# Two chunks of keys per product with v, longer prices for GpSimd and VectorE in the planner, and a new set of offsets, in a fused attention and two-MLP kernel

## The chip, the cores and the metric

The kernel runs on one core of one Trainium2 chip. The time is the device time of one execution in microseconds. Six views of the hardware occur below: PE is TensorE's matmul, PEld its weight load, DVE is VectorE, ACT is ScalarE, POOL is GpSimd and SP is SyncE, which issues all DMAs.

## The reference

Attention over 4 batches of 12 heads (448 positions, 64 channels), with an RMS norm on q and k, and then two gated MLPs without a residual, all in fp32:

```python
q_n, k_n = rmsnorm(q, g_q), rmsnorm(k, g_k)
scores = matmul(q_n, k_n.T) / sqrt(64)
attn = exp(scores - max(scores)); attn = attn / (sum(attn) + 1e-9)
x = matmul(attn, v)                    # -> 1792 tokens x 768
x = ((x @ w_a) * (x @ w_b)) @ w_out    # 768 -> 1536 -> 768
h = x @ w_in                           # 768 -> 2048
return (h * clip(h + 3, 0, 6) / 6) @ w_out2
```

## The kernel before

Products of the MLPs are made of fp32r matmuls on a value split in two: a high part (ACT rounds it) and a low part (the rest, a subtraction on DVE or POOL). Three matmuls of 128x128 by 448 columns make one exact product. Attention runs pair by pair of heads (`pair`, 24 pairs in four batches of six): scores for seven chunks of queries (L533, L534), exponentials on ACT, then the scaled probabilities `p` are turned by PE (L571, L585 to L588) into `pt`, whose copies out of PSUM go to ACT or DVE (L408, L412), and `value` (L598) multiplies them with `rv`. There are four chunks of keys, k = 0 to 3, so four `value` steps per pair; each is one matmul for the lower and one for the upper head of the pair, 64 columns of weights each, in plain fp32, which the profiler records as four matmuls. The last chunk has 64 rows per head. There are two `pt` buffers.

From about 80 us on, the MLP work of the batches that are done is laid between the attention of the later ones: `layer` for the first half of the tokens (L691 to L693). From about 816 us on only MLP is left: `layer7` (L964), which makes each 2x2 block product out of seven instead of eight; its weight sums (L922), its low halves (L397) and its output sums (L972) are DVE and POOL work. The first such layer ends and the second begins at about 1053 us.

The order on every engine is made at build time by the class `Plan`. Each operation is added with a due time, a cost per engine that may run it, and the tiles that it reads and writes. `run` then steps through planned time: each engine takes the operation with the earliest due time that is ready and whose buffers are free; an operation that several engines can do is taken by the first one listed, or by another when that one is busy for more than `LW` ns or the operation is late by more than a number in `LB` or `LF`. Costs that are marked as shared keep DVE and POOL from running at the same planned time. What comes out is one fixed list for each engine; on the chip, semaphores make an instruction wait where its inputs are late.

The tables of numbers at the top are the due times: `T` and `TQ` (start and pace of each batch), `R` (start and rate of each MLP stage), `OA` to `OD` (steps of a pair), `OW`, `LEAD` (weights of `layer`), `LW7`, `LX7` (how far ahead of a product `layer7` loads, sums and splits). `on_pool` and `on_dve` are the planned costs.

Of the kernel before, what the change touches and what calls it, by code (L numbers as in the profile page):

```python
# [19 lines left out]
NB, NH, S, D = 4, 12, 448, 64  # L20
# [5 lines left out]
PH = DM // 2  # L26
# [1 line left out]

T = (6.793, 78.0, 255.0, 440.0)
TQ = (1.45, 3.637, 4.75, 4.118)
R = ((85.0, 1.515), (255.0, 1.267), (411.278, 1.34), (703.581, 1.0), (943.0, 1.0))


BS = ((2, 3, 4), (1, 2, 3, 4), (2, 3, 4), (3, 4))
# [18 lines left out]

LB = (
    (548.658, 276.261, 561.206), (548.658, 402.965, 561.206), (548.658, 402.965, 561.206),
    (735.919, 402.965, 561.206),  # L60
)
LF = (
    (548.658, 402.965, 561.206), (548.658, 402.965, 561.206), (548.658, 402.965, 561.206),
    (548.658, -149.766, 561.206),
)
LW = 112.877


OA = (-7.027, -5.631, -5.6, -5.526, -4.903, -4.8, -4.475, -4.381)
OB = (-4.0, -2.7, -3.2, -2.3, -2.579, -2.6, -2.385)  # L70
OC = (0.0, -0.24, 0.482, 0.457, 4.632, 4.519)
UT = 5.13
UK = 2.0
OD = (0.4, 1.972, 3.0)


LEAD = 21.868
OW = (-9.089, -9.23, 1.129, 3.002, -1.607)
AFTER = 2.571


SLICE = (3, 3, 2)
# [4 lines left out]


MM = 206.7
LW7 = (34.0, 25.0, 20.0, 18.0)  # L90

SLICE7 = ((3, 3), (3, 3, 2))
XLEAD, XSTEP = -14.0, 3.7
LX7 = (20.0, 19.0, 18.5)


def piece_order(up, down, n, k):
# [49 lines left out]
class Plan:  # L149
# [16 lines left out]
    def add(self, due, cost, fn, reads=(), writes=(), after=()):  # L166


        o = Op()
        o.due, o.fn, o.idx = due * 1000.0, fn, len(self.ops)  # L170
        o.late = self.late
        o.cost = {e: c if isinstance(c, tuple) else (c, e == "G") for e, c in cost.items()}
        o.succ, o.need, o.ready = [], 0, 0.0
        o.bufs = []
        deps = {id(d): d for d in after}
        for k in reads:
            if k in self.last:
                deps[id(self.last[k])] = self.last[k]
        for k in writes:
            if k in self.last:  # L180
                deps[id(self.last[k])] = self.last[k]
            for d in self.readers.pop(k, ()):
                deps[id(d)] = d
        for k in reads:
            self.readers.setdefault(k, []).append(o)
        for k in writes:
            self.last[k] = o
        seen = set()
        for k in (*reads, *writes):
            b = k[0] if isinstance(k, tuple) else k  # L190
            if isinstance(b, Buf) and id(b) not in seen:
                seen.add(id(b))
                o.bufs.append(b)
                b.left += 1
        deps.pop(id(o), None)
        for d in deps.values():
            d.succ.append(o)
        o.need = len(deps)
        self.ops.append(o)
        return o  # L200

    def run(self, engines):
# [22 lines left out]
        while True:  # L225
            again = True
            while again:
                again = False
                for e in queue:
# [3 lines left out]
                    for key in queue[e]:  # L233
# [7 lines left out]
                        first = next(iter(o.cost))  # L241
                        if e != first and now < o.due + o.late[e] and free[first] <= now + LW:
                            continue
# [66 lines left out]


def on_pool(n):
    return (146 + 2.11 * n, True)


@with_exitstack
def fused_kernel(ctx: ExitStack, tc: tile.TileContext, nat, qt, gs_in, wpk, outT):
    nc = tc.nc
    V, A, G, SP = nc.vector, nc.scalar, nc.gpsimd, nc.sync
# [70 lines left out]
    def bank(role, ids, ordered=True):  # L390
        return Buf([banks[i] for i in ids], lines.setdefault(role, []) if ordered else None)

    plan = Plan()
    add = plan.add
# [23 lines left out]
    def pair(n0):  # L418
# [3 lines left out]
        b, h = divmod(n0, NH)  # L422
        plan.late = dict(zip("VAG", LB[b]))
        t0, q = T[b] + 4 * TQ[b] * h, TQ[b]
        lower, upper = slice(0, D), slice(D, P)

        def at(u):
            return t0 + q * u

        def at_chunk(j):  # L430
# [4 lines left out]
        rn, rv, sq, kc, ms, rstd, nt, sums, rs = [  # L435
            buf(k) for k in ("rn", "rv", "sq", "kc", "ms", "rstd", "nt", "sums", "rs")]
# [5 lines left out]
        for i, (lo, hi, who) in enumerate(alike):  # L442
            add(at(-10.7 + i), {"SP": 90 * (hi - lo)}, lambda e, lo=lo, hi=hi: e.dma_start(
                out=rn.t[:, lo:hi].rearrange("p c d -> p (c d)"), in_=nat[n0 // 2][:, lo * D:hi * D]),
                writes=[(rn, k) for k in who])
        for i in range(2):
            add(at(-8.9 + (4 * i if n0 else 0)), {"SP": 640}, lambda e, i=i: e.dma_start(out=rqs[i].t, in_=qt[n0 + i]),
                writes=[rqs[i]])
        add(at(-2.0), {"SP": 640}, lambda e: e.dma_start(
            out=rv.t.rearrange("p c d -> p (c d)"), in_=nat[n0 // 2][:, 14 * D:]), writes=[rv])  # L450
        for i, (lo, hi, who) in enumerate(alike):
            n, sl = (hi - lo) * D, slice(lo, hi)
            x, y, z, m, sk = [[(o, k) for k in who] for o in (rn, rstd, nt, ms, sq)]

            def square(e, sl=sl):
# [5 lines left out]
            cost = {"V": (on_dve(n), True), "A": on_act(n), "G": on_pool(n)}  # L461
            add(at(OA[0]), {k: cost[k] for k in ("VAA"[i] if n0 == 0 else SQ[b])}, square,
                reads=x, writes=sk)
            add(at(OA[1]), {"V": on_dve(n)}, lambda e, sl=sl: e.reduce_sum(out=ms.t[:, sl], in_=sq.t[:, sl], axis=AX.X),
                reads=sk, writes=m)
# [3 lines left out]
                reads=m, writes=y)  # L469
            add(at(OA[4]), {"A": 100}, lambda e, sl=sl: e.activation(rstd.t[:, sl], rstd.t[:, sl], AF.Exp, scale=-0.5),  # L470
                writes=y)
# [4 lines left out]
                reads=y, writes=z)  # L476
            add(at(OA[7]), {"V": 80}, lambda e, sl=sl: e.scalar_tensor_tensor(
                out=rstd.t[:, sl], in0=nt.t[:, sl], scalar=1.5, in1=rstd.t[:, sl], op0=ALU.add, op1=ALU.mult),
                reads=z, writes=y)
        for i in range(2):  # L480
            kcl, n, c0 = kcols[i], 4 - i, 4 * i
# [6 lines left out]
                reads=[y], writes=[(rn, f"{i}k")])  # L488
# [4 lines left out]
                reads=[(rn, f"{i}k"), (kc, i, 0)], writes=[(kc, i, 1)])  # L493
            tk = bank("t", BT[b], False)

            def turn_k(e, i=i, tk=tk):
# [14 lines left out]
                reads=[tk], writes=[kks[i]])  # L511

            def qhigh(e, i=i):
# [6 lines left out]
                reads=[rqs[i], "gg"], writes=[qhs[i]])  # L520
            add(at(OB[6] + 4 * i), {"V": (596, True)}, lambda e, i=i: e.scalar_tensor_tensor(
                out=qls[i].t[:, own_q[i]], in0=rqs[i].t, scalar=gg[:, 0:1], in1=f32(qhs[i].t[:, own_q[i]]), op0=ALU.mult, op1=ALU.subtract),
                reads=[rqs[i], qhs[i], "gg"], writes=[qls[i]])
        ps = []
        for j in range(NCK):
# [10 lines left out]
            u = j * 8 / NCK  # L536
# [20 lines left out]
        for j in range(0 if LATE[b] else NCK):  # L557
            opts = {"V": (363, True), "G": (617, True), "A": 560}
            add(at(4 + OC[5] + 0.15 * j), {k: opts[k] for k in NORM[b][j // 2]}, lambda e, j=j: norm(e, j),
                reads=[rs], writes=[ps[j]])  # L560
        pv = bank("v", BV[b])
        for k in range(4):
            pt = buf("pt")
            u = 4 + UT + k * UK
            if k < 3:
                for i, n in enumerate((4, 3)):
                    t = bank("t", BT[b], False)

                    def turn_p(e, k=k, i=i, n=n, t=t):
                        for c in range(n):  # L570
                            e.transpose(t.t[:, c * P:(c + 1) * P], ps[4 * i + c].t[:, k * P:(k + 1) * P], ident)  # L571

                    add(at(u + 0.5 * UK * i), {"PE": 109 * n}, turn_p, writes=[t, (pt, i)],
                        reads=["ident", *ps[4 * i:4 * i + n]])
                    cost = copy_ps(n * P)
                    add(at(u + 0.5 * UK * i + OD[0]), {x: cost[x] for x in PT[b]}, lambda e, i=i, n=n, t=t, pt=pt: copy(
                        e, pt.t[:, 4 * P * i:(4 * i + n) * P], t.t[:, :n * P]), reads=[t], writes=[(pt, i)])
                own = slice(0, P), slice(0, P)
                at_v, cols = (k, 4 + k), (0, S)
            else:  # L580
                t = bank("t", BT[b], False)

                def turn_rest(e, t=t):
                    for c in range(4):
                        e.transpose(t.t[:, c * P:(c + 1) * P], ps[3 + c].t[:, S - P:], ident)  # L585
                    for c in range(3):
                        e.transpose(t.t[lower, c * P:(c + 1) * P], ps[c].t[:, S - D:], ident)  # L587
                    e.transpose(t.t[lower, 3 * P:S], ps[3].t[lower, S - D:], ident[lower, lower])  # L588

                add(at(u), {"PE": 820}, turn_rest, reads=["ident", *ps], writes=[t, (pt, 0)])  # L590
                cost = copy_ps(4 * P)
                add(at(u + OD[0]), {x: cost[x] for x in PT[b]}, lambda e, t=t, pt=pt: copy(
                    e, pt.t[:, :4 * P], t.t), reads=[t], writes=[(pt, 0)])
                own, at_v, cols = (lower, upper), (3, 3), (0, D)

            def value(e, k=k, pt=pt, own=own, at_v=at_v, cols=cols):
                for i, rows in enumerate((lower, upper)):
                    e.matmul(pv.t[rows, :S], rv.t[own[i], at_v[i]], pt.t[own[i], cols[i]:cols[i] + S],  # L598
                             start=k == 0, stop=k == 3)

            add(at(u + OD[1]), {"PE": 930}, value, reads=[(pt, 0), (pt, 1), rv], writes=[pv])
        m, due = h // 2, at(u + OD[2])
        if LATE[b]:
            rb, eb = bank("t", BT[b], False), buf("tmp", "e")
# [17 lines left out]
        if b < GB:  # L622
            add(due, {"A": 424}, lambda e: e.activation(xx[:, m, b, 0], pv.t[:, :S], AF.Copy),
                reads=[pv], writes=[("xh", m, b)])
            add(due + 0.2, {"V": 535}, lambda e: sub(e, xx[:, m, b, 1], pv.t[:, :S], f32(xx[:, m, b, 0])),
                reads=[pv, ("xh", m, b)], writes=[("xl", m, b)])
            if n0 >= GHEAD - 4:
                tails.append(plan.ops[-1])
        else:
            add(due, {"A": 424, "V": 535}, lambda e: copy(e, xf[:, m, b - GB], pv.t[:, :S]),  # L630
                reads=[pv], writes=[("xf", m, b - GB)], after=tails)
# [246 lines left out]
    def layer7(no, ids, clock, late, finish):  # L878
# [223 lines left out]
        writes=["gg"])  # L1102
    add(0.2, {"V": 80}, lambda e: e.tensor_scalar(
        out=gg[:, 0:1], in0=gg[:, 0:1], scalar1=float(D) ** -0.5, scalar2=None, op0=ALU.mult), writes=["gg"])
    for k, sl in (("0", slice(S, 4 * P)), ("1", slice(0, D))):
        for x in ("qh", "ql"):
            t = K[x + k][0].tile
# [12 lines left out]

    layer(0, (0,), BM[0], pace(*R[0]), SLICE[0], LF[0])
    layer(0, (1,), BM[1], pace(*R[1]), SLICE[1], LF[0])
    ends[:] = [add(690.0, {"G": (1, False)}, switch, after=ends)]
    first_x = x_maker(xf, lambda m, bi: ("xf", m, bi), R[3][0], ends, held)
    layer(1, (0, 1), BM[2], pace(*R[2]), SLICE[2], LF[2], lambda k, due: first_x(XORDER[k], due))
    layer7(0, BM[3], pace(*R[3]), LF[2], x_maker(acc, lambda m, bi: ("acc", m, bi), R[4][0]))
    layer7(1, BM[4], pace(*R[4]), LF[3], lambda mb, due: put(mb[0], GB + mb[1], due))
    with tc.manual_schedule():
# [52 lines left out]
```

## Time and profile before

| what | value |
|---|---|
| median of 3 runs | 1277.68 us (1277.48 to 1277.71) |
| the profiled execution | 1274.44 us, its span 1272.7 us |
| PE busy, PEld busy | 97%, 82% of the span |
| DVE, ACT, POOL busy | 81%, 53%, 20% |
| granted TensorE clock, mean | 0.999 |

The span runs from the first to the last instruction; 1.7 us lie outside of it. A matmul's record overlaps the next one's, so the pace of PE is read from the distance of starts, and its waits from the idle time that is put down to a releaser.

### The profile page before, as it was taken

Reading aid. Unit: us, or ns where it says so; the run is one execution under the profiler, and the core shown is the slowest. Engines: PE = TensorE matmul, PEld = TensorE weight load, DVE = VectorE, ACT = ScalarE, POOL = GpSimd, SP = SyncE. Lnnn points to the kernel's source line nnn. Section 1 sums busy time; section 2 is a strip of 40 time slices with the busy share of each in tenths; the row PEclk is TensorE's granted clock in tenths of the full one; section 3 lists DMA queues with packets and bytes.
Section 4 is the critical chain, followed back from the end, with each engine's and each line's share of the span. In section 5 each row is a group of like instructions: output and inputs, shape, how many; then the busy total and the mean of one; then the engine's idle time right before and its main releaser. Section 6 shows DMA issues by size and latency. Waiting matters only on the chain.

```text
span 1272.7 us, 18366 instructions
## 1 busy us (share of the span) xinstructions
PE 1236.0 (97%) x6342; PEld 1039.3 (82%) x6342; DVE 1027.8 (81%) x1859; ACT 668.9 (53%) x1428; POOL 258.0 (20%) x281
## 2 busy tenths in 40 slices
PE   5999999999999999999999999999999999899998
PEld 3668777777988887888778878899899888799897
DVE  8999998997557798877878775876877799977977
ACT  7996766677235564654767643522422245534432
POOL 4331102212000021110121000522212234413131
PEclk9999999999999999999999999999999999999999
DMA  6456676765687587656646353655355445255433
GB/s 203 139 187 227 215 257 203 281 228 197 216 274 241 173 314 252 207 177 227 205 142 209 122 173 108 232 155 162 121 176 158 132 129 182 85 178 157 131 107 123
DMA packets 107853, 235.57 MB, mean 185 GB/s; under 512 B 9200, under 2 KB 74096, under 8 KB 107760
## 3 DMA queue, kind: packets, MB, share of 16 engines
q1 hardware_dynamic: 107760, 234.39, 56.2%
q8 instruction: 50, 0.82, 0.3%
q14 instruction: 43, 0.35, 0.1%
HBM read 162.01 MB, written 72.35 MB: 184 GB/s over the span
## 4 chain that ended last, share of the span: by engine, by line
PE 73%; DVE 15%; DMA 5%; issue 4%; ACT 2%; POOL 1%; SPq 0%; DVEq 0%; POOLq 0%; ACTq 0%
PE bank L964 26%; PE bank L691 10%; PE bank L693 10%; PE bank L692 10%; PE bank L598 5%; PE bank L571 4%; DMA wst<-in_w_dram 3%; PE bank L533 3%; PE bank L534 2%; DVE act L397 2%; DVE w L397 2%; DMA rn<-in_nat_dram 1%; PE bank L498 1%; DVE wf L649 1%; DVE acc L972 1%
## 5 line engine op out<-in xcount | busy, mean ns | idle before, releaser
L691 PE MATMUL bank<-xx,w 128*128 128x448 f32 x480 | 182.3, 380 | 1.1 <-DVE act L397 0.9
L693 PE MATMUL bank<-xx,w 128*128 128x448 f32 x480 | 175.5, 366 | 0.0
L692 PE MATMUL bank<-xx,w 128*128 128x448 f32 x480 | 175.4, 365 | 0.0
L964 PE MATMUL bank<-act,w 128*128 128x448 f32 x711 | 155.0, 366 | 6.0 <-DVE acc L972 4.1
L964 PEld LDWEIGHTS bank<-act,w 128*128 128x128 f32 x711 | 133.0, 188 | 18.9 <-ACT w L899 4.4
L964 PE MATMUL bank<-xx,w 128*128 128x448 f32 x612 | 132.1, 366 | 0.8 <-DVE acc L972 0.8
L691 PE MATMUL bank<-act,w 128*128 128x448 f32 x336 | 127.7, 380 | 2.6 <-DVE act L397 1.9
L673 ACT ACTIVATE w<-wf 128x768 fp32r<-128x768 f32 x104 | 85.6, 840 | 78.9 <-PE bank L692 64.8
L964 PEld LDWEIGHTS bank<-xx,w 128*128 128x128 f32 x612 | 114.9, 188 | 10.8 <-DVE acc L972 1.2
L693 PE MATMUL bank<-act,w 128*128 128x448 f32 x336 | 122.8, 366 | 0.0
L692 PE MATMUL bank<-act,w 128*128 128x448 f32 x336 | 122.7, 365 | 0.0
L397 DVE TENSOR_TENSOR w<-wf,w 128x384 fp32r<-128x384 f32 x185 | 101.3, 584 | 18.9 <-ACT w L673 15.8
L797 DVE TENSOR_TENSOR acc<-bank,acc 128x448 f32<-128x448 f32 x120 | 74.3, 622 | 48.4 <-PE bank L693 48.0
L539 DVE TENSOR_REDUCE nm<-bank 128x1 f32<-128x448 f32 x168 | 102.4, 618 | 13.0 <-PE bank L534 8.3
L543 ACT ACTIVATE p<-bank,nm,rstd 128x448 f32<-128x448 f32 x131 | 94.5, 724 | 27.5 <-PE bank L587 17.0
L408 ACT ACTIVATE pt<-bank 128x512 f32<-128x512 f32 (+1 forms) x131 | 71.4, 547 | 61.7 <-PE bank L571 51.4
L397 POOL TENSOR_TENSOR w<-wf,w 128x384 fp32r<-128x384 f32 x48 | 55.0, 1154 | 230.4 <-ACT w L673 224.8
L691 PEld LDWEIGHTS bank<-xx,w 128*128 128x128 f32 x480 | 90.2, 188 | 12.6 <-DVE act L397 1.7
L693 PEld LDWEIGHTS bank<-xx,w 128*128 128x128 f32 x480 | 90.1, 188 | 7.7
L692 PEld LDWEIGHTS bank<-xx,w 128*128 128x128 f32 x480 | 90.4, 188 | 6.2
L598 PE MATMUL bank<-pt,rv 128*64 128x448 f32 (+1 forms) x384 | 92.5, 563 | 0.5 <-DVE act L397 0.5
L964 PE MATMUL bank<-xt,w 128*128 128x448 f32 x405 | 89.7, 368 | 3.1 <-DVE xf L412 3.1
(214 smaller groups left out, 2487.4 us busy)
## 6 DMA issues: line engine op xcount, KB each, us to landing
wst<-in_w_dram SPq DMA_DIRECT2D x68, 768.0 KB, 5.9
split<-w SPq DMA_DIRECT2D x102, 384.0 KB, 3.7
w<-split SPq DMA_DIRECT2D x85, 384.0 KB, 3.9
kept<-wf SPq DMA_DIRECT2D x68, 384.0 KB, 3.0
wf<-kept SPq DMA_DIRECT2D x65, 384.0 KB, 4.2
wst<-kept SPq DMA_DIRECT2D x39, 384.0 KB, 3.6
rq<-in_qt_dram SPq DMA_DIRECT2D x48, 224.0 KB, 3.4
rn<-in_nat_dram SPq DMA_DIRECT2D x23, 448.0 KB, 4.1
```

The costliest lines, as they stand in the source:

```text
L397: e.tensor_tensor(out=out, in0=a, in1=b, op=ALU.subtract)
L408: A.activation(out, in_, AF.Copy)
L539: add(at(u + OC[1]), {"V": 531}, lambda e, s=s, nm=nm: e.tensor_reduce(out=nm.t, in_=s.t[:, :S], axis=AX.X, op=ALU.max, negate=True), read ...
L543: add(at(u + OC[3]), {"A": 704}, lambda e, j=j, s=s, nm=nm, p=p: e.activation(p.t, s.t[:, :S], AF.Exp, bias=nm.t, scale=rstd.t[:, qcol[j]: ...
L571: e.transpose(t.t[:, c * P:(c + 1) * P], ps[4 * i + c].t[:, k * P:(k + 1) * P], ident)
L598: e.matmul(pv.t[rows, :S], rv.t[own[i], at_v[i]], pt.t[own[i], cols[i]:cols[i] + S], start=k == 0, stop=k == 3)
L673: add(due - LEAD + OW[2], {"A": on_act(DM)}, lambda e: e.activation(w.t[:, 0], wf.t.bitcast(F32), AF.Copy), reads=both, writes=[(w, 0, 0), ...
L691: e.matmul(ps, w.t[:, 0, wsl], xh, start=start, stop=False)
L692: e.matmul(ps, w.t[:, 0, wsl], xl, start=False, stop=False)
L693: e.matmul(ps, w.t[:, 1, wsl], xh, start=False, stop=stop)
L797: add(due, {"V": 535}, lambda e, m=m, bi=bi, ps=ps: e.tensor_tensor(out=acc[:, m, bi], in0=ps.t[:, :S], in1=acc[:, m, bi], op=ALU.add), re ...
L964: e.matmul(out, w.t[:, a, chunk(c)], x, start=first and j + k == 0, stop=j + k == n + 1, skip_group_check=not first)
```

## The change

`value` now takes two chunks: for k = 0 and 2 the buffer is only noted, and at k = 1 and 3 one step is added that makes the four matmuls of both, with a planned cost of 1750 ns (two steps of 930 ns before). It reads both `pt` buffers. In `add`, every cost on DVE is multiplied by 1.03; in `on_pool`, operations of 384 and more columns cost 1.25 times as much. The tables of due times and the limits `LB`, `LF`, `LW` have new values. No arithmetic is added or taken away.

```diff
-T = (6.793, 78.0, 255.0, 440.0)
+T = (6.793, 74.014, 253.235, 440.0)
...
-R = ((85.0, 1.515), (255.0, 1.267), (411.278, 1.34), (703.581, 1.0), (943.0, 1.0))
+R = ((85.0, 1.74), (255.0, 1.196), (411.278, 1.34), (703.581, 1.0), (932.169, 1.0))
...
-LW = 112.877
+LW = 161.162
...
-LW7 = (34.0, 25.0, 20.0, 18.0)
+LW7 = (26.748, 25.0, 29.204, 19.253)
...
+        if "V" in o.cost:
+            o.cost["V"] = o.cost["V"][0] * 1.03, o.cost["V"][1]
...
-    return (146 + 2.11 * n, True)
+    return ((146 + 2.11 * n) * (1.25 if n >= PH else 1.0), True)
...
+        pts = []
         for k in range(4):
...
-            def value(e, k=k, pt=pt, own=own, at_v=at_v, cols=cols):
-                for i, rows in enumerate((lower, upper)):
-                    e.matmul(pv.t[rows, :S], rv.t[own[i], at_v[i]], pt.t[own[i], cols[i]:cols[i] + S],
-                             start=k == 0, stop=k == 3)
-
-            add(at(u + OD[1]), {"PE": 930}, value, reads=[(pt, 0), (pt, 1), rv], writes=[pv])
+            pts.append((k, pt, own, at_v, cols))
+            if k % 2 == 0:
+                continue
+
+            def value(e, two=tuple(pts)):
+                for k, pt, own, at_v, cols in two:
+                    for i, rows in enumerate((lower, upper)):
+                        e.matmul(pv.t[rows, :S], rv.t[own[i], at_v[i]], pt.t[own[i], cols[i]:cols[i] + S],
+                                 start=k == 0, stop=k == 3)
+
+            add(at(u + OD[1]), {"PE": 1750}, value, reads=[rv, *((t[1], x) for t in pts for x in range(2))], writes=[pv])
+            pts = []
```

**The place of `value` on PE.** The rows are the second pair of heads, whose v is `rv_257`, at its first two chunks; `kk`, `qh`, `ql` belong to scores, `ident` to the turning of probabilities, `identr` to that of keys. Before:

```order
L533 MATMUL bank_67<-kk_265,qh_261 128x448
L534 MATMUL bank_67<-kk_265,ql_263 128x448
L598 MATMUL bank_70<-pt_273,rv_257 64x448 x2
L533 MATMUL bank_65<-kk_265,qh_261 128x448
L534 MATMUL bank_65<-kk_265,ql_263 128x448
L598 MATMUL bank_70<-pt_274,rv_257 64x448 x2
L571 MATMUL bank_63<-ident,xf 128x128 x4
```

And now:

```order
L529 MATMUL bank_67<-kk_265,qh_261 128x448
L530 MATMUL bank_67<-kk_265,ql_263 128x448
L494 MATMUL bank_69<-identr,kc_259 128x64
L494 MATMUL bank_69<-identr,kc_259 128x128 x3
L612 MATMUL bank_63<-ident,rs_229 64x128 x6
L612 MATMUL bank_63<-ident,rs_229 64x64 x2
L600 MATMUL bank_64<-pt_273,rv_257 64x448 x2
L600 MATMUL bank_64<-pt_274,rv_257 64x448 x2
L529 MATMUL bank_65<-kk_265,qh_261 128x448
L530 MATMUL bank_65<-kk_265,ql_263 128x448
```

The two chunks stand next to each other, and other work has moved out from between them. Over the whole program the 96 chunk products of PE stand in 90 places before (84 alone, six in twos) and in 48 now, always two together.

**Where the second MLP begins, on PE.** `act` are the last output products of the first `layer7`, `xx` the first products of the second one, which read what DVE sums and splits out of the former. Before, from about 1047 us on:

```order
L964 MATMUL bank_65<-act_241,wb_6817 128x448 x3
L964 MATMUL bank_65<-act_242,w_237 128x448 x3
L964 MATMUL bank_65<-act_243,w_238 128x448 x3
L964 MATMUL bank_64<-act_241,wb_6817 128x448 x3
L964 MATMUL bank_64<-act_242,w_237 128x448 x3
L964 MATMUL bank_64<-act_243,w_238 128x448 x3
L964 MATMUL bank_63<-xx,w_238 128x448 x9
L964 MATMUL bank_64<-xx,w_237 128x448 x9
L964 MATMUL bank_65<-xx,w_239 128x448 x9
```

And now:

```order
L967 MATMUL bank_66<-xx,w_238 128x448 x9
L967 MATMUL bank_63<-act_241,wb_6859 128x448 x3
L967 MATMUL bank_63<-act_242,w_237 128x448 x3
L967 MATMUL bank_63<-act_243,w_238 128x448 x3
L967 MATMUL bank_67<-xx,w_237 128x448 x9
L967 MATMUL bank_64<-act_241,wb_6859 128x448 x3
L967 MATMUL bank_64<-act_242,w_237 128x448 x3
L967 MATMUL bank_64<-act_243,w_238 128x448 x3
L967 MATMUL bank_63<-xx,w_239 128x448 x9
L967 MATMUL bank_65<-act_241,wb_6859 128x448 x3
```

Three products of the new layer now stand between the last three of the old one.

**POOL in the middle of the second MLP** (the products that run from 1138 to about 1168 us before). `ws`, `wst`, `wf` are sums of weights, `w` and `wb` low halves of weights, `act` and `tmp` activations. Before, these are all:

```order
L397 TENSOR_TENSOR act_241<-tmpx_6826,act_241 128x448
L397 TENSOR_TENSOR tmp_247<-tmp_247,tmpx_6826 128x448
L397 TENSOR_TENSOR wb_6818<-wst_232,wb_6818 128x384
L397 TENSOR_TENSOR act_242<-xf,act_242 128x448
```

And now, in the same stretch:

```order
L925 TENSOR_TENSOR ws_6862<-wst_232 128x384
L393 TENSOR_TENSOR w_240<-ws_6862,w_240 128x384
L925 TENSOR_TENSOR ws_6861<-wf_234,wst_232 128x384
L393 TENSOR_TENSOR act_241<-tmpx_6868,act_241 128x448
L925 TENSOR_TENSOR wf_234<-ws_6861,wf_234 128x384
L393 TENSOR_TENSOR tmp_247<-tmp_247,tmpx_6868 128x448
L393 TENSOR_TENSOR w_237<-ws_6863,w_237 128x384
L925 TENSOR_TENSOR ws_6863<-wst_232 128x384
L393 TENSOR_TENSOR w_239<-ws_6863,w_239 128x384
L925 TENSOR_TENSOR ws_6862<-wf_235,wst_232 128x384
L393 TENSOR_TENSOR act_242<-xf,act_242 128x448
```

Sums and low halves of weights have come over from DVE. Counted over the program, 79 instructions leave DVE (1859 to 1780) and 77 come to POOL (279 to 356); 65 of them are such sums and halves of 384 columns (DVE 365 to 300, POOL 115 to 180).

## Rows read from the trace of the kernel before

**Rows 1.** The page, busy time of each engine.
```profile
PE 1236.0 (97%) x6342; PEld 1039.3 (82%) x6342; DVE 1027.8 (81%) x1859; ACT 668.9 (53%) x1428; POOL 258.0 (20%) x281
```

**Rows 2.** The page, chain that ended last, by engine.
```profile
PE 73%; DVE 15%; DMA 5%; issue 4%; ACT 2%; POOL 1%; SPq 0%; DVEq 0%; POOLq 0%; ACTq 0%
```

**Rows 3.** Stretches: length, busy time of PE, PEld, DVE, ACT, POOL, clock.
```profile
30.00:100.00 70.00, 70.00 (x478) 44.48 (x477) 66.47 (x131) 62.89 (x167) 23.76 (x42) 1.00 0.53 164
100.00:250.00 150.00, 147.31 (x763) 118.85 (x762) 138.57 (x258) 101.79 (x218) 25.38 (x30) 1.00 0.69 235
```

**Rows 4.** Timeline of PE, one chunk alone: start, length, instruction.
```profile
65.95 0.36 PE L533 MATMUL bank<-kk,qh 128*128 128x448 f32 x1
66.15 0.37 PE L534 MATMUL bank<-kk,ql 128*128 128x448 f32 x1
66.45 0.97 PE L598 MATMUL bank<-pt,rv 128*64 128x448 f32 x4
67.35 0.47 PE L533 MATMUL bank<-kk,qh 128*128 128x448 f32 x1
67.67 0.37 PE L534 MATMUL bank<-kk,ql 128*128 128x448 f32 x1
```

**Rows 5.** Timeline of PE, chunks 2 and 3 together.
```profile
59.81 0.37 PE L534 MATMUL bank<-kk,ql 128*128 128x448 f32 x1
60.10 1.87 PE L598 MATMUL bank<-pt,rv 128*64 128x448 f32 x8
61.91 0.55 PE L609 MATMUL bank<-ident,rs 128*64 128x128 f32 x6
```

**Rows 6.** Timeline of PEld, the second chunk of rows 5.
```profile
61.01 0.19 PEld L598 LDWEIGHTS bank<-pt,rv 64*64 64x64 f32 x4 [0.70 <-DVE nm L539]
```

**Rows 7.** Timeline of PE, chunks 0 and 1 together.
```profile
678.38 1.72 PE L598 MATMUL bank<-pt,rv 128*64 128x448 f32 x8
680.04 0.66 PE L571 MATMUL bank<-ident,p 128*128 128x128 f32 x4
```

**Rows 8.** Stretches, columns as in rows 3, around the MLPs' seam.
```profile
999.80:1109.10 109.30, 99.97 (x479) 90.45 (x478) 103.58 (x158) 51.94 (x101) 48.12 (x39) 0.98 0.44 134
934.10:999.80 65.70, 65.70 (x326) 60.88 (x325) 42.39 (x72) 14.18 (x28) 8.96 (x8) 1.00 0.57 163
```

**Rows 9.** Timeline of PE at three waits (idle time, releaser in brackets).
```profile
1025.42 0.44 PE L964 MATMUL bank<-act,w 128*128 128x448 f32 x1 [2.47 <-DVE acc L972]
...
1055.69 2.50 PE L964 MATMUL bank<-xx,w 128*128 128x448 f32 x11 [0.84 <-DVE acc L972]
...
1091.62 2.70 PE L964 MATMUL bank<-xt,w 128*128 128x448 f32 x9 [3.10 <-DVE xf L412]
1094.12 3.00 PE L964 MATMUL bank<-xx,wb 128*128 128x448 f32 x9
1096.96 2.02 PE L964 MATMUL bank<-act,w 128*128 128x448 f32 x9
```

**Rows 10.** DVE groups from 1000 to 1110 us: count, busy time, mean.
```profile
L397 DVE TENSOR_TENSOR act<-xf,act 128x448 fp32r<-128x448 f32 x16 | 13.8, 887 | 0.8 <-ACT act L1039 0.6
...
L397 DVE TENSOR_TENSOR act<-tmpx,act 128x448 fp32r<-128x448 f32 x5 | 5.7, 1136 | 0.1
```

**Rows 11.** Groups over the whole run, columns as in rows 10.
```profile
L397 DVE TENSOR_TENSOR w<-wf,w 128x384 fp32r<-128x384 f32 x185 | 101.3, 584 | 18.9 <-ACT w L673 15.8 <-ACT w L899 1.6
...
L397 DVE TENSOR_TENSOR act<-bank,act 128x448 fp32r<-128x448 f32 x56 | 34.6, 617 | 4.2 <-ACT act L700 3.8
...
L408 ACT ACTIVATE pt<-bank 128x512 f32<-128x512 f32 x73 | 43.4, 594 | 42.4 <-PE bank L571 32.3 <-PE bank L588 9.7
...
L397 POOL TENSOR_TENSOR w<-wf,w 128x384 fp32r<-128x384 f32 x48 | 55.0, 1154 | 230.4 <-ACT w L673 224.8 <-PE bank L534 2.6 <-ACT rstd L468 1.7
```

**Rows 12.** Timeline of DVE beside POOL's next row.
```profile
1021.23 1.57 DVE L397 TENSOR_TENSOR act<-xf,act 128x448 fp32r<-128x448 f32 x1
```

**Rows 13.** Timeline of POOL there.
```profile
1020.85 1.47 POOL L397 TENSOR_TENSOR tmp<-tmpx,tmp 128x448 f32<-128x448 f32 x1 [2.10 <-DVE tmpx L397]
```

More of the change, by code (lines that the diff above doesn't have):

```diff
@@ L26 @@
 PH = DM // 2
-T = (6.793, 78.0, 255.0, 440.0)
-TQ = (1.45, 3.637, 4.75, 4.118)
-R = ((85.0, 1.515), (255.0, 1.267), (411.278, 1.34), (703.581, 1.0), (943.0, 1.0))
+T = (6.793, 74.014, 253.235, 440.0)
+TQ = (1.436, 3.637, 4.788, 4.218)
+R = ((85.0, 1.74), (255.0, 1.196), (411.278, 1.34), (703.581, 1.0), (932.169, 1.0))
 BS = ((2, 3, 4), (1, 2, 3, 4), (2, 3, 4), (3, 4))
@@ L54 @@
 LATE = (True, False, False, False)
[L58 to L65, printed above, removed]
-LW = 112.877
-OA = (-7.027, -5.631, -5.6, -5.526, -4.903, -4.8, -4.475, -4.381)
-OB = (-4.0, -2.7, -3.2, -2.3, -2.579, -2.6, -2.385)
-OC = (0.0, -0.24, 0.482, 0.457, 4.632, 4.519)
+LB = ((344.344, 276.261, 561.206), (548.658, 402.965, 561.206), (548.658, 402.965, 561.206), (606.623, 311.013, 561.206))
+LF = ((548.658, 394.053, 761.141), (548.658, 402.965, 561.206), (548.658, 402.965, 561.206), (553.891, -149.766, 668.974))
+LW = 161.162
+OA = (-7.027, -5.631, -5.6, -5.311, -5.026, -4.8, -4.475, -4.381)
+OB = (-4.77, -2.7, -3.245, -2.3, -2.091, -2.6, -2.386)
+OC = (0.104, -0.677, 0.482, 0.457, 4.632, 4.519)
 UT = 5.13
@@ L77 @@
 LEAD = 21.868
-OW = (-9.089, -9.23, 1.129, 3.002, -1.607)
-AFTER = 2.571
+OW = (-8.493, -9.23, 1.129, 3.002, -1.61)
+AFTER = 2.346
 SLICE = (3, 3, 2)
@@ L89 @@
 MM = 206.7
-LW7 = (34.0, 25.0, 20.0, 18.0)
+LW7 = (26.748, 25.0, 29.204, 19.253)
 SLICE7 = ((3, 3), (3, 3, 2))
 XLEAD, XSTEP = -14.0, 3.7
-LX7 = (20.0, 19.0, 18.5)
+LX7 = (10.733, 19.0, 18.5)
 def piece_order(up, down, n, k):
```

## The prediction

> **What bounds the kernel now.** I read the page first, then the chain, then stretches, then single rows. PE is busy 97% of the span, and 73% of the chain that ended last is PE, 15% DVE [rows 1, 2]. So a nanosecond taken from PE's list counts, unless another engine sets the pace where it is taken. By stretches: from 30 to 250 us PE is busy 217.3 of 220 us, but DVE is nearly as full: 66.5 of 70 us, then 138.6 of 150 [rows 3]. The one long stretch where PE clearly loses time is 999.8 to 1109.1 us, the end of the first and the start of the second MLP: DVE is busy 103.6 of 109.3 us and PE waits for it, up to 3.1 us at once [rows 8, 9]. At the pace of the stretch ahead of it, 65.7 us for 326 matmuls or 0.2015 us each, its 479 matmuls would take 96.5 us; 12.8 us are lost there. Part of that is the pace itself: the granted clock of the stretch is 0.98, and after the 3.1 us wait two products of nine matmuls take 2.50 and 2.84 us from start to start [rows 9] where 9 x 0.2015 is 1.81, so 1.7 us went on a lower clock.
>
> **Two chunks in one step.** This is PE work, and the rows price it. Two neighbouring score matmuls start 0.20 us apart. Ahead of a chunk that stands alone the distance is 0.30, and the chunk takes 0.90 us to the next start [rows 4]; so one alone costs 0.90 + 0.10 = 1.00, two alone 2.00 us. Chunks 2 and 3 together (the second has the shape of 64 rows, [rows 6]) start 0.29 after their predecessor and take 1.81: 1.90 us, saving 0.10. Chunks 0 and 1 together take 1.66; with the same 0.09 ahead 1.75, saving 0.25 [rows 5, 7]. In other words a stop on each change of kind is paid once, and two chunks of 128 rows also run into each other. Of the 24 couples of each sort, two of the first and four of the second already stand together before (one of each in [rows 5, 7]). The change therefore gives 22 x 0.25 + 20 x 0.10 = 5.5 + 2.0 = **7.5 us** less PE work. Another 0.12 us goes with each chunk whose next matmul is a score (0.32 instead of 0.20 between the L533 and L534 behind it, [rows 4]); which neighbours come is a matter of the new order, and I count nothing for it (at most 42 x 0.12 = 5 us, likely 1).
>
> What could take it back: a couple must wait for both copies out of PSUM, and both `pt` buffers stay taken until it is done, so the copies for chunks 2 and 3 start later. Behind a waiting couple stand scores and turned probabilities of the next pair, and MLP matmuls. In the new order the couples stand further behind the turning that feeds them than the single chunks did: at least about ten short matmuls or scores lie between, where before it was as few as five. Ten of these last about 2 us, and the copy takes ACT 0.594 us [rows 11]. I cost this wait at nothing; if the cover is gone at every couple, 48 times 0.3 us (the size of a stop at a change of kind) is 14 us, the far end.
>
> **New prices and offsets.** They add no work; they choose engines and order. 65 sums and low halves of weights go from DVE to POOL. At 0.584 us each that is 38 us less on DVE, and at 1.154 us 75 us more on POOL [rows 11], which was busy 258 of 1272.7 us [rows 1]. DVE's relief only shows where PE waits for DVE. Between the same PE products I counted the instructions in both orders and priced them with their mean durations: in the tight stretch (999.8 to 1109.1 us) DVE gets 106.4 us of work before and 107.8 us after, POOL 48.0 before and 40.4 after. So the relief is elsewhere: 10 us in 100 to 225 us, 11 us in 1138.2 to 1176.6 us. Less POOL work in the tight stretch helps DVE a little, since DVE is held up beside it: the same subtraction that takes 617 ns with its source in PSUM takes 887 and 1136 ns there with its source in SBUF [rows 10, 11], 16 x 0.27 + 5 x 0.52 = 6.9 us on 48.1 us of POOL; 7.6 us less POOL is 1.1 us less of that. It cancels the 1.4 us more. The tight stretch should then stay as long as it is, but for the new order at its seam: three products of the new layer stand between the last of the old one, so that PE has work while DVE makes the first operands, and the wait of 0.84 us at 1055.69 us [rows 9] has cover. I take **1.0 us** for it (with the restart of PE behind it). Bounds: all 12.8 us of the stretch gained, or the three longest waits of rival C added.
>
> For the rest of the list (first 30 us, short waits in the attention) the trace gives no sign; I take zero, and 3 us either way.
>
> The sum, against the profiled execution: 1274.4 - 7.5 - 1.0 = 1265.9 us. The median of the runs is 3.2 us above that execution, so 1277.7 - 8.5 = **1269.2 us**.
>
> **The rivals.**
>
> A. *The tight stretch dissolves.* The planner now believes that DVE and POOL take longer (1.154 us for a POOL row, where 0.956 was planned and 1.195 now), so it may place what PE needs earlier, and DVE waits less beside POOL. For it: 6.9 us of holding up, POOL work down by 7.6 us, and the seam woven. Against it: the DVE work itself is not less. At its full size, 1277.7 - 7.5 - 12.8 = 1257.4 us; at half, 1264.
>
> B. *DVE sets the pace where PE is relieved.* Half of the pairs, and so half of the 7.5 us, lie before 250 us, where DVE is 92 to 95% busy [rows 3]. If DVE is the bound there, only 3.7 us remain, and without the gain at the seam the time is 1274; a few stray waits more make it 1276. Against it: DVE gets 10 us less to do in 100 to 225 us. For it: what goes to POOL can come back as waiting. One such case stands in [rows 12, 13]: the DVE subtraction ends just as the POOL one does and takes 1.57 us where 0.617 is the time of the same subtraction from PSUM [rows 11]. If each of the 15 more POOL instructions in that stretch cost DVE 0.96 us, that is 14 us, more than the 10 us that it gains. The Trainium skill says the same as a rule (SBUF — State Buffer, section "SBUF: two separate sides"): DVE and GpSimd share one pair of ports under an exclusive lock, and the loser blocks for the whole instruction. By that rule moving work from DVE to POOL need not help DVE; the trace agrees with the lock in those two rows, and does not tell from two rows how often it strikes.
>
> C. *Slower: the woven seam makes PE wait.* PE takes its list in order. If DVE is late with the operands of the `xx` products that now stand ahead of the last `act` products, PE stops, and the `act` products behind it, whose sums DVE has to add before the next operands, stop as well. The order shows three such products ahead of the old layer's end; at 3.1 us each, the longest wait in [rows 9], that is 9.3 us, and two of them may bring the 1.7 us of lower clock again: 1277.7 - 7.5 + 9.3 + 3.4 = 1282.9 us. It decides the sign from 7.5 us of new waits on. For it: DVE is full there. Against it: these operands were due 11 us later before, and DVE's list is ordered by the same due times.
>
> D. *It does not do what it says.* Excluded by the order: 48 couples, none apart.
>
> **How the numbers follow.** A difference under 0.2% (2.6 us) can hardly be told from no change. The forecast (1265 to 1273) gets 0.48, A (1257 to 1265) 0.20, B 0.18 (0.08 of it below 1275.1, 0.10 within 0.2%), C (1280.3 and more) 0.12, and 0.02 I put below A. Faster is then 0.48 + 0.20 + 0.02 + 0.08 = 0.78, same 0.10, slower 0.12. The range takes in A, the forecast and B and a little of C: 1257 to 1281.
>
> **What would show it.** In the profile after: 48 places of L600 with eight records each, half of them about 1.66 us and half 1.81 us to the next start; the same 384 records. The stretch up to about 816 us (the first L967 product) is then some 7 us shorter. POOL is busy about 330 us, DVE about 980. The stretch between the two MLPs stays at 105 to 110 us with DVE over 90% busy. I am wrong if the couples show idle time put down to the `pt` copies, if the first L967 product starts at 816 us again (B), or if the `xx` products at the seam wait (C).

## The result and the profile after

The changed kernel takes 1261.06 us (median of 4 runs, 1259.76 to 1262.94) against 1277.58 us; the ratio is 0.9879, 95% interval 0.9863 to 0.9895. That is 16.5 us less, inside the predicted range, but twice the 8.5 us that the sum gave. The two profiled executions, 1274.44 and 1262.94 us, lie only 11.5 us apart; what is known of the rest of the difference is told at the end.

The page of the changed kernel, busy time (rows 1 answer for before):

```profile
PE 1230.1 (98%) x6342; PEld 1041.7 (83%) x6342; DVE 993.4 (79%) x1780; ACT 674.7 (54%) x1430; POOL 341.5 (27%) x358
```

DVE is busy 34 us less and POOL 83 us more. Now the run in four stretches, cut at the same matmuls of PE: the first one, the first of `layer7`, two in the middle of it about 100 us apart (the seam of the two MLPs lies between), the last one. The stretches are called head, middle, seam and last stretch below. Before (columns as in [rows 3]; the seam is the first row of [rows 8]):

```profile
8.30:816.60 808.30, 795.79 (x4200) 636.84 (x4201) 652.92 (x1220) 496.22 (x1095) 138.15 (x177) 1.00 0.61 206
816.60:999.80 183.20, 182.46 (x893) 167.12 (x892) 135.89 (x233) 56.11 (x109) 33.85 (x29) 1.00 0.55 165
...
1109.10:1268.30 159.20, 157.35 (x774) 144.89 (x773) 130.60 (x226) 61.09 (x117) 37.17 (x31) 1.00 0.44 136
```

And after:

```profile
8.40:806.70 798.30, 789.98 (x4201) 641.17 (x4202) 642.88 (x1179) 501.75 (x1093) 169.31 (x212) 1.00 0.61 209
806.70:988.90 182.20, 181.03 (x892) 167.13 (x891) 124.76 (x217) 55.50 (x109) 61.51 (x49) 1.00 0.52 165
988.90:1091.40 102.50, 98.39 (x478) 89.05 (x478) 96.08 (x159) 53.61 (x104) 42.39 (x33) 1.00 0.45 143
1091.40:1257.10 165.70, 160.32 (x775) 144.31 (x774) 124.76 (x202) 60.29 (x116) 67.56 (x58) 1.00 0.41 131
```

So the change is four things in one: the head is 10.0 us shorter, the middle 1.0, the seam 6.8, and the last stretch is 6.5 us longer. Of the head's 10.0 us, 5.8 are less busy time of PE (795.79 to 789.98) and 4.2 are less idle time (12.5 to 8.3).

The couples look as foretold: 48 places of eight records, the 24 of chunks 0 and 1 with 1.65 us to the next start in the median, the 24 of chunks 2 and 3 with 1.80. Chunks 2 and 3 in the timeline of PE, to be read beside [rows 5]:

```profile
48.61 0.36 PE L530 MATMUL bank<-kk,ql 128*128 128x448 f32 x1
48.90 1.87 PE L600 MATMUL bank<-pt,rv 128*64 128x448 f32 x8
50.70 0.47 PE L529 MATMUL bank<-kk,qh 128*128 128x448 f32 x1
```

Chunks 0 and 1, beside [rows 7]:

```profile
360.61 0.37 PE L696 MATMUL bank<-xx,w 128*128 128x448 f32 x1
360.91 1.72 PE L600 MATMUL bank<-pt,rv 128*64 128x448 f32 x8
362.56 0.47 PE L694 MATMUL bank<-xx,w 128*128 128x448 f32 x1
362.87 0.36 PE L695 MATMUL bank<-xx,w 128*128 128x448 f32 x1
```

1.80 and 1.65 us to the next start, with 0.29 and 0.30 ahead, as in [rows 5, 7]. Behind the couple the distance from the first matmul to the second is 0.31 instead of 0.20 again: the stop on the way out, which [rows 4] showed and the sum counted as nothing.

### The profile page after: what moved, and what is told of

Its sections match the earlier page's. It is cut to its first block, busy times and chain, and to the rows that moved or that the text cites. A ratio compares the mean times of both kernels' runs of the same rounds, so it can differ in the third digit from the quotient of the medians.

```text
span 1261.0 us, 18450 instructions
## 1 busy us (share of the span) xinstructions
PE 1230.1 (98%) x6342; PEld 1041.7 (83%) x6342; DVE 993.4 (79%) x1780; ACT 674.7 (54%) x1430; POOL 341.5 (27%) x358
## 5 line engine op out<-in xcount | busy, mean ns | idle before, releaser
L967 PEld LDWEIGHTS bank<-act,w 128*128 128x128 f32 x729 | 135.7, 188 | 25.2 <-ACT w L902 4.2
L393 POOL TENSOR_TENSOR w<-wf,w 128x384 fp32r<-128x384 f32 x73 | 78.8, 1091 | 275.1 <-ACT w L676 229.5
L967 PEld LDWEIGHTS bank<-xx,w 128*128 128x128 f32 x576 | 108.1, 188 | 9.1 <-DVE xf L408 0.3
L694 PEld LDWEIGHTS bank<-xx,w 128*128 128x128 f32 x480 | 90.2, 188 | 16.8 <-issue 7.8
L393 DVE TENSOR_TENSOR w<-wf,w 128x384 fp32r<-128x384 f32 x161 | 90.1, 594 | 10.7 <-ACT w L676 8.3
L696 PEld LDWEIGHTS bank<-xx,w 128*128 128x128 f32 x480 | 90.1, 188 | 7.9
L695 PEld LDWEIGHTS bank<-xx,w 128*128 128x128 f32 x480 | 90.4, 188 | 6.1
L967 PE MATMUL bank<-xt,w 128*128 128x448 f32 x423 | 92.6, 366 | 0.0
L600 PE MATMUL bank<-pt,rv 128*64 128x448 f32 (+1 forms) x384 | 86.2, 557 | 0.0
```

The costliest lines, as they stand in the source:

```text
L393: e.tensor_tensor(out=out, in0=a, in1=b, op=ALU.subtract)
L694: e.matmul(ps, w.t[:, 0, wsl], xh, start=start, stop=False)
L695: e.matmul(ps, w.t[:, 0, wsl], xl, start=False, stop=False)
L696: e.matmul(ps, w.t[:, 1, wsl], xh, start=False, stop=stop)
L967: e.matmul(out, w.t[:, a, chunk(c)], x, start=first and j + k == 0, stop=j + k == n + 1, skip_group_check=not first)
```

## Experiments: which of the four comes from what

All times are medians; the ratios are against the kernel before on the same chip.

**Couples taken apart, with nothing else moved.** The changed kernel's plan is made as it is; only when the instructions are written out, the second chunk of a couple is held back until PE's next planned step is out, or, where another step needs it sooner, until just ahead of that one. One couple stays together, so there are 95 places.

```diff
-            def value(e, two=tuple(pts)):
+            def value(e, two=tuple(pts[:1])):
...
+            both.second = lambda e, value=value, two=tuple(pts[1:]): value(e, two)
...
+                        if e == "PE" and kept:
+                            self.flush(engines["PE"])
+                        if hasattr(o, "second"):
+                            self.held = o, mine
```

> The changed kernel with its own plan, every engine's list as it is, except that on PE the second chunk of each couple is issued one PE step later (95 places instead of 48). Theory 1 (the stop at each change of kind and the run-on of two 128-row chunks are paid by PE): 47 couples apart cost 24 x 0.25 + 23 x 0.10 = 8.3 us, so 1261.1 + 8.3 = 1269.4 us. Rival (DVE sets the pace in the first 250 us, or other waits shrink by as much): half or less of it, 1261 to 1265 us.

Measured: 1272.87 us, ratio 0.9982 (0.9968 to 0.9997). That is more than theory 1 said. Its head, and one of its chunks with what stands around it:

```profile
7.80:817.70 809.90, 798.78 (x4201) 636.69 (x4202) 644.23 (x1180) 503.86 (x1093) 168.12 (x212) 1.00 0.61 206
```

```profile
365.44 0.37 PE L711 MATMUL bank<-xx,w 128*128 128x448 f32 x1
365.73 0.97 PE L614 MATMUL bank<-pt,rv 128*64 128x448 f32 x4
366.63 0.47 PE L709 MATMUL bank<-xx,w 128*128 128x448 f32 x1
366.95 0.36 PE L710 MATMUL bank<-xx,w 128*128 128x448 f32 x1
```

The head is 11.6 us longer than with couples (809.9 against 798.3), and the other three engines' lists are the same, instruction by instruction. 8.8 us of it are more busy time of PE (798.78 against 789.98); 2.8 us are more idle time, most of it in two waits, with couples and then without:

```profile
PE bank L694 <- DVE acc L800: 0.3, 1, 0.3
PE bank L529 <- ACT p L539: 2.3, 3, 1.0
```

```profile
PE bank L709 <- DVE acc L815: 1.9, 1, 1.9
PE bank L543 <- ACT p L553: 3.7, 6, 1.2
```

From start to start over all places, the way in costs 3.9 us more than with couples and the chunks themselves 3.7, where the sum of the prediction has 8.3 for 47 couples. The way out costs 3.4 us more: 0.11 us for each of 10 added exits ahead of an fp32r matmul (366.63 to 366.95 is 0.32) and about half of that for each of 37 ahead of turned probabilities or keys. These are 11.0 us, and the other matmuls of the head take 2.3 us less, for a reason that the trace does not show. So PE does pay for the stops, and DVE does not set the pace: the rival falls.

**Couples alone.** The kernel before with the new `value` step and nothing else.

> The kernel before with couples alone; old prices and old tables. Theory 1: 7.5 us less PE work and nothing else, 1277.6 - 7.5 = 1270 us. Rival (the new order brings the gain, couples alone lose it to waits for both copies): 1276 us or more.

Measured: 1271.29 us, ratio 0.9973 (0.9962 to 0.9984). Its head and its seam:

```profile
7.80:809.10 801.30, 790.36 (x4201) 641.46 (x4202) 651.86 (x1211) 497.86 (x1098) 147.63 (x183) 1.00 0.62 208
991.20:1102.30 111.10, 102.11 (x479) 91.68 (x478) 103.94 (x158) 52.16 (x101) 48.15 (x39) 0.97 0.42 132
```

The head gives 7.0 us, 5.4 of them busy time of PE (795.79 to 790.36); the seam is 1.8 us longer than before, at a granted clock of 0.97. The head bears theory 1 out. In the medians 3.4 to 4.2 us are left of it, about midway between the two theories; the seam, which has no couples, blurs them (see the end).

**The other way round: no couples, the rest of the change.**

```diff
-            add(at(u + OD[1]), {"PE": 1750}, value, reads=[rv, *((t[1], x) for t in pts for x in range(2))], writes=[pv])
+            add(at(u + OD[1]), {"PE": 930}, value, reads=[(pt, 0), (pt, 1), rv], writes=[pv])
```

> The changed kernel with one chunk per step again (930 ns planned each); new prices and tables stay. Theory 1: the couples' 7.5 us come back, 1261.1 + 7.5 = 1268.6 us, and the other 9 us of the gain stay. Rival (couples give all of it): 1277 us. Second rival (couples give nothing): 1261 us.

Measured: 1274.23 us, ratio 0.9991 (0.9977 to 1.0005). The head is 812.7 us, 14.4 us longer than with couples. 10.1 us of that are busy time of PE, with one fall of the granted clock to its lower level among them, and 4.3 are idle time, so the couples' own part is less than 14.4. The seam:

```profile
1002.70:1105.60 102.90, 98.44 (x480) 89.08 (x479) 96.53 (x159) 53.72 (x104) 41.96 (x33) 1.00 0.46 142
```

102.9 us: the shorter seam does not need the couples. Without them the rest of the change is worth nothing in total: a head 4.4 us longer than before and a last stretch 3.7 us longer (162.9) use up the seam's gain.

**The tables alone.** All new numbers, old prices, single chunks. The lines show what is taken out of the prices of the changed kernel; `value` is single as in the run above.

```diff
-    return ((146 + 2.11 * n) * (1.25 if n >= PH else 1.0), True)
+    return (146 + 2.11 * n, True)
...
-        if "V" in o.cost:
-            o.cost["V"] = o.cost["V"][0] * 1.03, o.cost["V"][1]
```

> The kernel before with the new tables (T, TQ, R, LB, LF, LW, OA to OD, OW, AFTER, LW7, LX7) alone; old prices, single chunks. If the tables alone bring what the couples do not: 1277.6 - 9 = 1268.6 us. If they need the new prices to be of use: 1275 to 1280 us.

Measured: 1288.78 us, ratio 1.0117 (1.0089 to 1.0145): 1.2% slower than before, worse than both expectations. The seam takes 113.3 us at a clock of 0.95, the last stretch 166.8 at 0.98.

**Couples and tables, old prices.** The prices are taken out as above, and the couples stay.

> The changed kernel with the old prices (no 1.03 on DVE, no 1.25 on POOL); couples and new tables stay. Theory: the couples give 7.5 us up to the first layer7 product whatever the prices are, and the new tables without the prices cost as they did alone (16 us by the end), so about 1277 us. Rival (prices do nothing by themselves): 1261 us.

Measured: 1279.75 us, ratio 1.0017 (1.0002 to 1.0032), near the theory's 1277. The new prices are worth 1.4% in the changed kernel (0.9879 against 1.0017). This does not agree with the term that the prediction gave them. The next run has them alone.

**The prices alone.** The kernel before with `1.03` and `1.25` and nothing else.

> The kernel before with the new prices alone; old tables, single chunks. Theory: prices move some work between DVE and POOL and shake the order, PE's work is the same: 1274 to 1281 us up to noise, no couples' gain. Rival (prices alone bring the seam's 6 us): 1270 us.

Measured: 1266.36 us, ratio 0.9905 (0.9883 to 0.9927). The theory of the expectation falls: with two factors in the planner and no change in work, the kernel is 1% faster. The rival (the seam's 6 us) had the place right. Head 807.3, seam 101.7, last stretch 159.4 us:

```profile
999.60:1101.30 101.70, 98.65 (x478) 89.03 (x477) 96.02 (x161) 53.64 (x104) 42.55 (x32) 1.00 0.46 141
1101.30:1260.70 159.40, 158.21 (x774) 144.62 (x774) 120.23 (x203) 61.66 (x117) 63.06 (x56) 1.00 0.44 138
```

So the seam is theirs. In it DVE runs 161 instructions instead of 158 and is busy 96.0 us instead of 103.6; POOL runs 32 instead of 39. PE's idle time there falls from 9.3 us (109.30 - 99.97) to 3.1. DVE has not less to do but is held up less beside POOL. The groups of DVE there, against [rows 10]:

```profile
L399 DVE TENSOR_TENSOR act<-xf,act 128x448 fp32r<-128x448 f32 x13 | 11.1, 864 | 0.4 <-ACT act L1041 0.3
...
L399 DVE TENSOR_TENSOR w<-ws,w 128x384 fp32r<-128x384 f32 x11 | 5.9, 550 | 0.2
...
L399 DVE TENSOR_TENSOR act<-tmpx,act 128x448 fp32r<-128x448 f32 x5 | 3.9, 778 | 0.0
```

`act<-tmpx` went from 1136 to 778 ns; `w<-ws` is at 550 ns, where the same stretch of before has

```profile
L397 DVE TENSOR_TENSOR w<-ws,w 128x384 fp32r<-128x384 f32 x10 | 7.0, 702 | 0.0
```

The trace shows the holding-up record by record. Take DVE's sums and subtractions of 384 and 448 columns in the seam of before. With no operand in PSUM and no POOL instruction beside them they take 0.54 to 0.56 and 0.61 to 0.63 us. Of the 23 that start while a POOL instruction runs, 21 end 0.42 us (384 columns) or 0.48 us (448) behind the end of that POOL instruction, however long it has yet to run, as in [rows 12, 13]. With an operand in PSUM they take 0.61 to 0.63 us beside POOL as well. The lock that the prediction cited (the Trainium skill, SBUF — State Buffer, section "SBUF: two separate sides") is what this looks like. Held up by more than 0.1 us are 20 of them before, by 14.7 us together, and 13 with the prices, by 9.6. The rule says what a collision is; how many there are depends on the order.

**Which price.** `1.25` on POOL alone, and `1.03` on DVE alone, in the kernel before.

> The kernel before with the longer price for POOL (1.25 from 384 columns on) alone. Theory: it is this price that shortens the seam (999.8 to 1109.1 us of before), since the plan no longer sets DVE's and PE's work against POOL results that come 0.2 us late and DVE work into POOL's time: 7 us less there, 1269 us. Rival (the 1.03 on DVE does it): 1277 us.

> The kernel before with the longer price for DVE (1.03) alone. Theory (POOL's price does it): 1275 to 1278 us, the seam as long as before. Rival: the seam 7 us shorter, 1269 us.

Measured: 1271.64 us, 0.9976 (0.9957 to 0.9995), and 1273.18 us, 0.9982 (0.9965 to 1.0000). Their seams, POOL's price first:

```profile
1001.60:1109.40 107.80, 101.92 (x478) 91.83 (x477) 100.44 (x167) 53.45 (x102) 37.87 (x29) 0.97 0.43 136
```

```profile
1003.00:1106.70 103.70, 98.72 (x479) 88.92 (x478) 99.09 (x158) 53.88 (x104) 46.50 (x36) 1.00 0.44 140
```

My bet on POOL's price was wrong. DVE's 1.03 shortens the seam by 5.6 us, POOL's 1.25 by 1.5, both by 7.6. In the medians each gives about 0.2%, both 0.95%: DVE's price alone makes the head 3.8 us longer (812.1). Each of the two takes the POOL work in the seam down (37.9 and 46.5 us, from 48.1), yet the price with less POOL work there has the longer seam, so the amount of POOL work alone does not decide. The rest of the comparison is weak: POOL's price was profiled in the slowest of its ten runs (1278.33 us), with two falls of the clock in the seam, and its DVE has 167 instructions there. Its DVE is held up by 10.5 us, with DVE's price by 11.6, so that sum does not rank the two seams either. Which of the instructions held up are those that PE needs next was not taken apart.

**The weave at the seam.** The changed kernel with `R`'s last start at 943.0, and the kernel before with 932.169.

> The changed kernel with the start of the second layer7's due times put back from 932.169 to 943.0; PE's list is the same up to the seam and unwoven there. Theory: the weave of new-layer products between the last old-layer ones is what shortened the seam by 6.5 us (1052 to 1109 us of before), so these come back: 1261 + 6 = 1267 us, with everything up to the seam as in the changed kernel. Rival (the new prices shorten the seam): 1261 us.

> The kernel before with the second layer7's due times 11 us earlier (943.0 to 932.169) alone, which weaves its first products into the last of the old layer. The prediction's term: 1.0 us less. As the changed kernel lost nothing without the weave: no gain, 1277 us, up to 3 us more at the seam.

Measured: 1258.97 us, 0.9853 (0.9835 to 0.9872), and 1277.8 us, 1.0024 (1.0006 to 1.0043). Seams:

```profile
988.20:1090.40 102.20, 98.94 (x479) 90.63 (x478) 96.83 (x162) 53.75 (x104) 46.63 (x32) 0.98 0.46 143
```

```profile
998.00:1110.30 112.30, 102.29 (x479) 91.62 (x478) 104.62 (x161) 50.72 (x99) 47.38 (x38) 0.97 0.41 130
```

Unwoven, the changed kernel's seam stays at 102.2; woven, the old one's is 3 us longer, not 1 us shorter. The weave gains nothing at the seam, and where DVE is late it costs. In the old kernel's seam PE is idle 10.0 us instead of 9.3, and the granted clock falls twice instead of once, which is the larger part of the 3 us. In the changed kernel the old start makes the last stretch 3.6 us shorter (162.1 against 165.7 us), which the expectation did not look at, and the medians 2.1 us.

**The last stretch.** The changed kernel with the leads of before.

```diff
-LW7 = (26.748, 25.0, 29.204, 19.253)
+LW7 = (34.0, 25.0, 20.0, 18.0)
...
-LX7 = (10.733, 19.0, 18.5)
+LX7 = (20.0, 19.0, 18.5)
```

> The changed kernel with the old leads LW7 and LX7 of layer7 (loads 34, splits 20 and 18 us ahead; activations 20, 19, 18.5). Theory: the changed kernel loses 5.8 us against before in the last 130 us since these leads (loads 7 us later, first activation sums 9 us later) make operands late: the last stretch gets 5 us shorter, 1256 us. Rival (POOL's larger share there makes DVE wait): no change in the last stretch, 1261 us.

Measured: 1256.46 us, ratio 0.9832 (0.9815 to 0.9848), as the theory said, and the best of all. The last stretch takes 160.5 us instead of 165.7, and the ratio's interval lies below that of the change:

```profile
1090.30:1250.80 160.50, 158.63 (x775) 144.66 (x774) 120.78 (x203) 61.22 (x116) 62.95 (x56) 1.00 0.44 135
```

POOL is nearly as busy there (63.0 against 67.6 us, 37.2 before), so its larger share is not the cause, as the prices alone show too (63.1 us of POOL, 159.4 us). Who PE waits for there, first with the new leads, then with the old ones:

```profile
PE bank L967 <- DVE act L393: 2.3, 4, 0.6
PE bank L967 <- DVE acc L975: 1.6, 2, 1.3
PE bank L967 <- DVE xf L1023: 1.1, 1, 1.1
PE bank L967 <- issue: 0.3, 1, 0.3
```

```profile
PE bank L967 <- issue: 1.0, 1, 1.0
PE bank L967 <- DVE acc L975: 0.5, 1, 0.5
PE bank L967 <- DVE xf L1023: 0.4, 1, 0.4
```

The waits for low halves of activations (`act L393`) are gone, and 3.4 of the 5.2 us are less waiting. `LW7` and `LX7` were put back together; which of them does it was not tried.

**Both put back.** Old leads and the old start.

> The changed kernel with the old leads LW7 and LX7 and the old start 943.0 of the second layer7: couples, prices and the other tables stay. If the two gains add (4.6 us by the leads, 2 us by the start): 1254.5 us. If both take away the same late operands of the last 130 us: 1256 to 1257 us.

Measured: 1258.77 us, ratio 0.9874 (0.9854 to 0.9893). Its last stretch takes 160.6 us like that of the old leads alone, so the two gains do not add (5.2 us by the leads, 3.6 by the start, 5.1 by both); that it is not better than the old leads alone the stretches (799.0, 181.6, 102.8, 160.6) bear out. The ratio is even 0.4% behind, of which the profiled executions show 1.1 us; the rest is open.

The stretches of all profiled executions in one place (us):

| kernel | head | middle | seam | last |
|---|---|---|---|---|
| before | 808.3 | 183.2 | 109.3 | 159.2 |
| couples | 801.3 | 182.1 | 111.1 | 160.4 |
| tables | 812.9 | 183.0 | 113.3 | 166.8 |
| couples, tables | 804.7 | 181.9 | 111.7 | 165.9 |
| prices | 807.3 | 183.9 | 101.7 | 159.4 |
| POOL's price | 808.5 | 184.1 | 107.8 | 163.3 |
| DVE's price | 812.1 | 182.4 | 103.7 | 162.5 |
| weave | 807.3 | 182.1 | 112.3 | 159.7 |
| prices, tables | 812.7 | 182.4 | 102.9 | 162.9 |
| the change (all three) | 798.3 | 182.2 | 102.5 | 165.7 |
| the change, couples apart | 809.9 | 183.6 | 101.6 | 163.5 |
| the change, old leads | 799.0 | 182.0 | 101.9 | 160.5 |
| the change, unwoven | 798.3 | 181.4 | 102.2 | 162.1 |
| the change, both put back | 799.0 | 181.6 | 102.8 | 160.6 |

"The change" and "couples apart" have the same lists in the last three columns; they differ there by 0.9 to 2.2 us, which is how far single executions may be trusted. Read down the columns: the head follows the couples (798.3 to 804.7 us with them, 807.3 and more without), the seam the prices (101.6 to 102.9 with both, 107.8 and more without DVE's). The last stretch is less clear: with the new leads it takes 162.1 to 166.8 us, the old start takes more than half of their loss back as well, and with the old leads it is 159.2 to 160.6, but 162.5 and 163.3 in the kernels with one price alone, for a reason that stays open.

## Why the prediction was right, and where not

**Couples, 7.5 us: right in mechanism and, at the places themselves, in size.** By the distances of starts, the way in gives 3.8 us and the chunks themselves 3.6, together 7.4; with couples alone it is the same. The exits, of which the prediction says "I count nothing for it (at most 42 x 0.12 = 5 us, likely 1)", give 1.8: ahead of turned probabilities or keys there are 58 fewer, at half the price, and ahead of fp32r matmuls 16 more. That makes 9.2 us. But the other matmuls of the head take 3.4 us more, in the change as with couples alone, and why is open; so PE's busy time falls by 5.8 us. That the head is 10.0 us shorter is 4.2 us less waiting, which the prediction put at zero, 3 us either way, among the "short waits in the attention".

**The wait for both copies: right.** None of the 48 couples has idle time of PE ahead of it. In the head of the changed kernel PE waits 0.5 us in all for copies of probabilities out of PSUM (1.4 us before, 2.4 with couples alone), in two places, both of them matmuls that turn probabilities:

```profile
PE bank L582 <- ACT pt L404: 0.3, 1, 0.3
PE bank L568 <- ACT pt L404: 0.2, 1, 0.2
```

**New prices, zero: wrong.** "The tight stretch should then stay as long as it is" is the step that failed. I priced the holding-up of DVE by the amount of POOL work (6.9 us on 48.1 us), and so its change by 1.1 us. The two groups that I took were not half of it: over all of DVE's sums and subtractions of 384 and 448 columns it was 14.7 us, and in the changed kernel it is 8.7. The runs show a seam 7.6 us shorter with the prices alone, from an order in which DVE's work is not less and DVE and POOL collide less. [rows 12, 13] were read wrong, too: the DVE subtraction ends 0.48 us behind the POOL one, not with it. The rival "the tight stretch dissolves" had the place right and half of it came; I had given it 0.20 for want of a row that shows an order's collisions ahead of its run.

**The weave, 1.0 us: wrong.** It gains nothing at the seam of the changed kernel and costs 3 us there in the old one. The wait of 0.84 us that it covers [rows 9] was one of a stretch in which DVE was late anyway.

**The last stretch, zero: wrong.** 6.5 us lost. I looked at its DVE load (11 us lighter) and not at the leads, whose shortening from 20 to 10.7 and from 34 to 26.7 us stands in the change. The old leads take 5.2 us of it back, the old start by itself 3.6.

**The rivals B and C** did not come. DVE at 92 to 95% did not bind: taken apart, the couples made PE's list longer and the head with it. (What B puts at half of the chunks lies lower: 39 of 96 run before 250 us.) The `xx` products at the seam did not stop PE; the wait there stands before `act` products:

```profile
1032.52 3.91 PE L967 MATMUL bank<-act,w 128*128 128x448 f32 x18 [1.74 <-DVE acc L975]
1036.27 1.99 PE L967 MATMUL bank<-xx,w 128*128 128x448 f32 x9
1038.10 0.77 PE L967 MATMUL bank<-act,wb 128*128 128x448 f32 x3
```

So the total landed in the range partly by luck: 2.5 us too little for the head, 5.8 too little at the seam, and 6.5 us of loss that was not foreseen. What the medians gained beyond the two profiles had no term in the sum at all.

## To carry to other kernels

A list that one engine works off in order has a price for every change of kind, on the way in and on the way out; count the places, not the steps, and count both ends. Where a planner orders engines that get in each other's way, other prices can be worth as much as less work, and what they bring can't be read from sums of work: run them alone. When many numbers change at once, cut the run at the same instructions and compare stretch by stretch; a gain can hide a loss that is easily taken back, here 0.5% by two lines of leads.

## What the hardware showed

The holding-up of DVE beside POOL brings a second loss, by the clock. In the seam the granted clock of the profiled executions is 0.95 to 0.98 in every kernel without both prices but the one with DVE's alone (before 0.98, couples 0.97, tables 0.95, couples with tables 0.97, woven 0.97, POOL's price 0.97) and 1.00 with both, but for the unwoven one (0.98). Of the 13 falls to the lower level (1.2 instead of 2.4 GHz) in these seams each begins in a wait of PE of 2.2 to 3.1 us or within 1.4 us behind it; the wait of 2.47 us in [rows 9] brought none. The fall in [rows 9] cost 1.7 us. How many falls there are changes from execution to execution. Among 24 runs of the kernel before on one chip, the ones with a mean clock of 0.999 took 1273.4 us in the median (3 runs), those at 0.997 1275.5 (10) and at 0.996 1276.1 (7); among 25 on another, 1273.8 (6), 1276.7 (8) and 1276.2 (6). On a third chip the only one of 13 at 0.999 took 1278.6 us, so the clock is not all of it. The execution profiled before had little of it (0.999), which fits about 2 of the 5 us by which the two profiles lie closer than the medians; the profiled execution of the change, at 1.000, is 1.9 us above its own median, and that is not the clock. The four runs with the old leads, all at 1.000, lie within 0.23 us.
